# Sums with v in 128 columns of the sequence DFT's PSUM bank: one eviction for both, 120 epochs, seven score banks, a new order of work

## The chip, the cores and the metric

The kernel runs on one core of one Trainium2 chip. The metric is the device time of one launch in microseconds (us), the median of several runs. The core has TensorE (PE in the profile, its weight loads as PEld), VectorE (DVE), ScalarE (ACT), GpSimd (POOL), and DMA queues that are here mostly issued from SyncE (SP). TensorE writes its results to PSUM, which has eight banks of 512 float32 columns on 128 partitions.

## The reference, cut to what matters

Two branches read the same x (2048 tokens, 640 features) and are mixed by a gate. Branch A is a Fourier mixing layer: a DFT over the features and one over the sequence, real part only. Branch B is attention with 32 query heads of 20 features and one shared key and value head.

```python
g = sigmoid((x * gate_w).sum(-1, keepdims=True))
# branch A
a = einsum("bsd,ed->bse", x, dft_hid_re)
b = einsum("bsd,ed->bse", x, dft_hid_im)
y = einsum("ts,bse->bte", dft_seq_re, a) - einsum("ts,bse->bte", dft_seq_im, b)
# branch B, H = 32, Dh = 20
scores = einsum("bhqd,bkd->bhqk", q, k) * Dh ** -0.5
p = softmax(scores, axis=-1)
o = einsum("bhqk,bkd->bhqd", p, v) @ wo
out = g * y + (1 - g) * o
```

## The kernel before, in words

Float32 products are made of two-part operands (a rounded high part and a low part), so that most matmuls run in the fast float32 form. The program has three phases.

**Head.** Projections q, k, v and the gate, then the feature DFT (`ab`, line 137). The first maxima of scores run beside it.

**Main phase.** It runs the list `PLAN`, one character per piece of PE work, in the order in which PE gets it. Four kinds of work are woven together:

- `a`, line 356: a score tile (128 queries by 512 keys) for the softmax's maxima. VectorE reduces it to one column (line 363). There are 1888 in the list.
- `b`, line 824: a score tile transposed (128 keys by 512 queries), with the maximum already subtracted through two more rows. ScalarE takes the exponential into an SBUF tile `pt` (line 834). There are 1920 in the list. Sixteen `pt` tiles exist.
- `y`, line 698: half-height matmuls of the sequence DFT, 320 columns, made with a fast matrix scheme of seven products; a group of 96 half matmuls sums into the first 320 columns of one bank, `F0`. The list has 48 groups (4608 matmuls). At a group's end ScalarE copies the bank (line 726), and GpSimd adds it to what DRAM holds of y (line 753).
- `av`, line 838: the sums with v. One step takes four `pt` tiles (two heads, two query blocks of 512, the same 128 keys) and does four matmuls of 512 columns, each in its own 32 columns of the array, into one bank, `V`. Sixteen steps complete half of a pair of heads; ScalarE copies the bank (line 852, `finish_half`), DMAs write sums and denominators to DRAM.

A score of head 0 and a `y` with digit 0 use rows 0 to 63 of the array, those of head 1 and digit 1 use rows 64 to 127; below, the two halves are called the **two lanes**. A `y` in one lane and scores in the other run at the same time. `av` uses all 128 rows. In the list small letters are scores of head 0 and capitals those of head 1 (first the `a`, then the `b`; the letter's place gives the bank), `0` and `1` are a `y` in that lane, `V` is one `av` step, `-` ends a `y` group. Six banks `S0` to `S5` serve scores, one serves `av`, one serves `y`. Both lanes may not sum into the y bank at once, so a `y` that changes lane waits for a score's eviction behind the last `y` of the other lane (`Halves.run`).

**Tail.** The last 8 `y` groups use two banks and both lanes in turn, with the scores and sums of the last pair of heads between them; the output projection follows.

PE, ACT, DVE and POOL execute in the order in which the program is written; the list therefore also sets the order of the exponentials, the maxima and the copies. POOL also prepares the operands of the coming `y` group (lines 485, 495 and 496 for the DFT matrix, 523 to 527 for x).

Of the kernel before, what the change touches and what calls it, by code (L numbers as in the profile page):

```python
# [8 lines left out]
F32 = mybir.dt.float32  # L9
# [8 lines left out]
P = 128  # L18
S = 2048
# [15 lines left out]
def kernel(  # L35
# [151 lines left out]
    with ExitStack() as c1:  # L187
# [3 lines left out]
        rot = Rot(["B", "V", "F", "B", "F", "A", "A", "A"])  # L191
# [74 lines left out]
        warm = bank("V", "warm")  # L266
# [411 lines left out]
    class Halves:  # L678
# [11 lines left out]
        def run(self, g):  # L690
# [5 lines left out]
            start, stop = grp[k] == 0, grp[k] == (6 if one else 3) * NT - 1  # L696
            grp[k] += 1
            mm = nc.tensor.matmul(ps[g % len(ps)], w, woven(x), start=start, stop=stop)  # L698
            if one:

                if not start and self.last != g:
                    tc.add_manual_dep(mm.ins, self.mark.ins.name, ORDER, reason="turns with a bank")
                    known["PE"] = max(known["PE"], self.exp)
                if start:
                    known["PE"] = max(known["PE"], known["y"])
                self.last, self.mark = g, None
# [50 lines left out]

    def f_stream():
# [5 lines left out]
        for g, (n, k) in enumerate(GROUPS):  # L764
            ps = [bank("F0", f"y_{n}_{k}")[:, :HALF]]
            if g >= GMAIN:
                ps.append(bank("S5", f"y_{n}_{k}_1")[:, :HALF])
            y0 = y_in(n, k)
            grp = [0, 0]
            for sh in range(2):  # L770
                h, l = c_ops.pop((g, sh))
                load_c(g + 1, sh)
                for j in range(SJ):
# [12 lines left out]
                    if jj == NT - 1:  # L786
                        ended.append({"n": n, "k": k, "ps": ps, "y": y0})
# [11 lines left out]
    known = {"PE": -1, "ACT": -1, "y": -1}  # L799
# [36 lines left out]

    def av_mm(ps, g, t, kc, first, last):
        nc.tensor.matmul(ps[32 * g : 32 * g + 32, :], vsb[:, kc, :], t, start=first, stop=last)  # L838

    def av_step(p, qh, kc):  # L840
        if kc == 0:
            av[qh] = bank("V", f"av_{p}_{qh}")
# [7 lines left out]
    def finish_half(p, qh):  # L850
        ob = op.tile([P, ROW], F32, name="ob")
# [8 lines left out]
        if p == LAST:  # L860
            sm = op.tile([P, 16], F32, name="sm")
            ts = slice(qh * S // 2, (qh + 1) * S // 2)
            for hh in range(2):
                move(sm[64 * hh : 64 * hh + 64], sum_d[2 * p + hh, ts].rearrange("(s t) -> s t", t=16))
            later(4, finish_last, ts, sm)
        elif qh == 1:
            sm = op.tile([P, 32], F32, name="sm")
            move(sm, sum_d[2 * p : 2 * p + 2].rearrange("h (s t) -> (h s) t", t=32))
            later(24, finish_sums, p, sm)
# [11 lines left out]
    def finish_last(ts, sm):  # L881
# [13 lines left out]
    SCORES = "abcdefABCDEFghijklGHIJKL"  # L895
    PLAN = (
        "g1b111id11k1111l1a11hc1111d1k1111lAhCk00LD000A0H000K0I0F00D0000HA00KVJbgKCfVVlkCAHdV0KC00H00A000J00F"
        "0K0I00B00A0J0000K0F000IB0V0IF00HEajV1h11dk111a11lc11h111dk1111a1l1111bi11ej11-VdBiGKfVV1fk1111gb1c11"
        "1j1l1e1111g1111hdi11111f1k11a1dHVaKbFdIVVLbI0J000A00E00L000HC0000G00DE00L0000I00B0G00D00LE0VDlgBKcVA"
        "H0000E00I00D0LA00000B000KClDVV1i11dl11h11e1111a1id11111fe1h11iGVIf-HjeAV1f1h11e1g11d11i1l111b11e1g11"  # L900
        "c1d1111fh1V1HikDa1ViDhFEgV0H00FG00E00JI000000BF000GdEVVDlKGbcV0K00BG000I0F00JE0000000HA0I00L0D000E0H"
        "00A000CJ000FVVLc111a1jh1111e1l11c111j1ab11k11f111JiV-dhAEIfVVeI1a1l1bj111111e11i1l111g1111dbi111k11f"
        "VeHiDFgV11i1dGkFbVaJ00KF000H0C00G00D000EL0000H00CA000J00LVCjGfBeVVBl0GEC000J0000LB000000GE000J00I00L"
        "000BAVl1b11i11a111ej1111lh11111cgd111el1VfjACKbVVC-eAjHlVd1he1111gf1i1111j1h111e11a11i1111fj1e1111hG"
        "cVkBgLCdVgB000I0FJ000K0G0000BC0F000DVVL00C000J0A0H0000E0L0CJ0000GB00000FK000D0C000AH000KVVGc1k11d1h1"
        "1f111g111c1kd111111h1fg1cKV-ViElaBJV1fG1e1j1c11h11111fg1j1e11b111i1111g1l1dV1aL11dbiKVjClGBeVLc0H00A"
        "K0D00000L0CH0000A00K0J0000F0I0B000E00AD0VVG0E00JB0000I0000LA00K000DB0C00FgVVIal111h1d1e1111ia1111l11"
        "1j11b111iegF-VeIaBlJVfgK1d1Ch1VeJ1a11i1h1f111111je111i111ah1l1111dk11cVjFIKbaVVGe0H00C0FD00000A00K00"
        "B0CVVAj0B00K0L000C00DG000K00000H00FG0C00J00000E0H00FG00c0D0hKVbIf111j11k111ac111b1j111f1k1a1VVlB1g1e"
        "c1JV-EgdBIlVc1j11f1h11g1e1111i11d1fh1111g1e11i1111jh11fAVF0H000A0J0C00K00F0H0000000JAKcVAjeLIbVVBCkL"  # L910
        "gdV0E0L0C00J0000AH000EL000I0000D0BG000L00E00I00JA0VDegiFHV1ai111k11fh1111dg1111i1fe1111hd11VHeiFd-GV"
        "VAj111lc11e11h111aj1111li1b11111e1j111a1fiHVa11iHlkDVVK0F00J0000BI000GE0F000D00HC000AeVVI00AJ00000FK"
        "B00I000G0D00L0000EI0B000000AD00F0KVVGej1111b1lc1111g11e1j11b1l11111ia1e-JVaIBlKjVV1dkb1111l111g1c111"
        "1je111h111la1c111de11h11GlVadHClKVhA0LD000I00K00B000G00F000JC0B000EVVehCdGLVhE0G000C0J0F000H0E00G0I0"
        "0000D0F00H0EG000000IDViEa1Dl11hVa1h111d111l11kc111g11bd1f111kIVDeIb-fGVV1b1g1f1k11id1111b11g1lk11111"
        "c1111da111h11liEVfGBjiEVJ00B0I000E0GF00000J0B000C00E00GdFVVkCJ0AB000L00000E0I00J000GF00000HC00J00E0A"
        "00L0VVaLeJIbVJak1111cbl111j11111a1ei11l1111h1j1GcVVA-dIhKfVIahd111111l1k11c11g1b11j11f11c1111k1b1g11"
        "dl1VFBgcDkVV0I0E0J0000BG000F0C000K0D00H0GVBigDKfVA000JE00L0CH0000G000D0000KF0H000C0A000J0K00L00BVEaB"
        "1lj11iV1aj1111bif1111k111a1j11111bc-kFVVIeLbaJVf11h111dge1111i11f1h1111j11g1c11k11b1fV1e1bG1fIjVVJ00"
        "0FI00H0AE0000J00L0000I0AH000J0E000F0000GCVaFjKiBVlD0K0A0hC00000L0J000E0AB0000C00F0kDVVIe111fhg1d1111"  # L920
        "11i1e1h111la11d11c11kHVV-ihEJaFV1c11h11a1k11jf1111b11i11e1g1111j1l1c1111haVH0A0000I0F0J000E0H00G00C0"
        "0FJ0VJcFgBkVg0CF0eJH0VVE0HFj0cG0VdLBeIgVCj0B000G0E00L0ID000000AH00F0K000I00D00HVBl11d1ik1111a1f1h111"
        "11i1de11g1h111-fIVViLEbaJV1l1e111jb11g1c1l11111kd11b111g1f11c11kd111gVaL00IK0bDVbCeGjFVV00EJL0000C00"
        "AH0000K0D0L0I0000BG000E00JF0000H0C000G0K000D0F0B0000I000ADeVVgB1d11i11k1f11g111h1c1111d11e11lg1-IbVV"
        "1ch1a111k1l1111dc111h11g11k1f11j1111bcV1bD1kfiG1VcJeBlGVFi00K0AHD0000I0L00000E0G000B0J0CVVCbjgELVdIA"
        "0000H0K00F0I0D000H0G000EF00000ID0B00000E00AClVVkB1a1l111j1i11e111hf11111a11jec111HlVbeGDcL-VVJf111ei"
        "11g1b111j11f11ik1a111111h1j1f1i11ea11VCkJfAhVdIL000BG00E00000CJ00000FB000AEjVVA000H0D00K0F00I0A00H00"
        "J0K0000C000FH0G0000D00C0KVJgIeHlVVHc11g11fk11d111h11i1a11111f1ed111bG-iVViDBkaLVKd1bl111g1c11k111d1l"
        "111h1g11c11111e1d1l11h1cVbjFKcGVjBK0000F0I0A00J0000BE0L00CVVCKfHjaVkC0H0F0A0J000K00C0000H0000FJ0G00K"
        "0C0000B00D00F0G0I00EVVKfc1j111gh11111e1l11d1c111g11k1b11DlVV-jFhKcAV1h11c1k11lad11111h1i11e111a1l111"  # L930
# [77 lines left out]
    def next_v():  # L1008
        st = taken["V"] - LAG
        taken["V"] += 1  # L1010
        if st >= 0:
            av_step(*STEPS[st])
            if STEPS[st][2] == NT - 1:
                finish_half(*STEPS[st][:2])
# [114 lines left out]
```

## Time and profile before

| | |
|---|---|
| Runs shown | 1712.6, 1713.92, 1716.32 us; median 1713.92 us |
| Profiled execution, its own time | 1714.89 us |
| Its span in the trace | 1713.1 us |
| Granted TensorE clock | 1.0 of full speed in all 40 slices |
| PE / DVE / ACT / POOL busy share | 99% / 84% / 70% / 48% |

The profile has one row per group of instructions: the line, the engine, the operation, what it writes and reads, the count, the busy time of the group and the mean time of one. A float32 matmul of `av` leaves two records, one for each of its two passes, so 2048 matmuls of `av` stand as x4096. Records of PE overlap, since a record lasts from the start to the drain and the next matmul starts before that; the distance between starts is what counts.

In the views by time a row gives the start, the length from the first start to the last end, the engine and the group; what stands in square brackets at the end is idle time of that engine before the row and what ended it.

### The profile page before, as it was taken

What the parts mean: (1) busy time and instruction counts of PE and PEld (TensorE: products, weight loads), DVE (VectorE), ACT (ScalarE), POOL (GpSimd) and SP (SyncE); (2) the same over time, 40 slices, a digit from 0 to 9 for tenths busy, and PEclk for the clock granted to TensorE, in tenths of its full rate; (3) what the DMA queues carried; (4) which work ended last, traced back from release to release, by engine and by line L of the source; (5) the groups of instructions that cost most, each with busy time, mean ns of one, the idle gap of its engine ahead of it and who ended that gap; (6) DMA issues with size and microseconds to landing.
All of it is one profiled execution on the core that took longest, in us unless ns stands there. A gap on an engine that the chain in (4) does not pass through costs nothing.

```text
span 1713.1 us, 40813 instructions
## 1 busy us (share of the span) xinstructions
PE 1703.6 (99%) x16342; PEld 1194.6 (70%) x16342; DVE 1440.0 (84%) x2355; ACT 1199.3 (70%) x2337; POOL 817.6 (48%) x559
## 2 busy tenths in 40 slices
PE   9999999999999999999999999999999999999998
PEld 8899986666666666666666666666666666667788
DVE  5779999999898889898998989998989998855264
ACT  5732257777787777877777777778777777877731
POOL 1011344553646464647566565565564453542252
PEclk9999999999999999999999999999999999999999
DMA  8863433343344444435344544353443332325667
GB/s 292 240 182 117 141 109 122 103 134 106 121 136 138 122 134 126 141 110 165 128 144 135 170 126 138 115 151 116 139 145 118 99 111 89 107 79 182 200 214 248
DMA packets 131002, 243.88 MB, mean 142 GB/s; under 512 B 26356, under 2 KB 77556, under 8 KB 128292
## 3 DMA queue, kind: packets, MB, share of 16 engines
q1 hardware_dynamic: 130012, 238.00, 44.2%
q0 software_dynamic: 800, 3.28, 0.6%
q8 instruction: 128, 2.10, 0.5%
q14 instruction: 62, 0.51, 0.1%
HBM read 194.62 MB, written 50.86 MB: 143 GB/s over the span
## 4 chain that ended last, share of the span: by engine, by line
PE 90%; DMA 3%; issue 3%; POOL 2%; DVE 1%; SPq 0%; ACT 0%; POOLq 0%; DVEq 0%
PE av L838 27%; PE y L698 19%; PE a L356 16%; PE b L824 16%; PE ab L137 7%; PE q L126 1%; PE q L128 1%; PE q L127 1%; DMA oraw<-rx_d 1%; POOL ya L753 1%; POOL oraw L632 1%; SPq L118 0%; DMA out_dram<-oy 0%; PE o L128 0%; POOL yt L748 0%
## 5 line engine op out<-in xcount | busy, mean ns | idle before, releaser
L363 DVE TENSOR_REDUCE mx<-a 128x1 f32<-128x512 f32 x2048 | 1265.5, 681 | 126.4 <-PE a L356 88.5
L834 ACT ACTIVATE pt<-b 128x512 f32<-128x512 f32 x2048 | 1055.4, 613 | 291.7 <-PE b L824 171.8
L698 PE MATMUL y<-x,ch 64*128 64x320 f32 x3584 | 706.8, 299 | 0.9 <-ACT yt L726 0.9
L356 PE MATMUL a<-ks,qs 60*128 60x512 f32 x2048 | 705.1, 411 | 0.3 <-ACT half L570 0.3
L824 PE MATMUL b<-qs,ks 62*128 62x512 f32 x2048 | 672.2, 408 | 0.1
L698 PEld LDWEIGHTS y<-x,ch 64*128 64x128 f32 x3584 | 545.3, 186 | 51.0 <-issue 31.4
L838 PE MATMUL av<-pt,vsb 128*32 128x512 f32 x4096 | 512.8, 601 | 0.0
L698 PE MATMUL y<-x,cl 64*128 64x320 f32 x1792 | 496.1, 297 | 0.0
L356 PEld LDWEIGHTS a<-ks,qs 60*128 60x128 f32 x2048 | 345.8, 184 | 123.3 <-ACT pt L834 64.2
L824 PEld LDWEIGHTS b<-qs,ks 62*128 62x128 f32 x2048 | 336.9, 184 | 132.6 <-DVE mx L363 74.2
L485 POOL TENSOR_TENSOR craw<-craw 128x1024 f32<-128x1024 f32 x80 | 189.4, 2368 | 266.3 <-DMA craw<-in_cre_dram 116.2
L698 PEld LDWEIGHTS y<-x,cl 64*128 64x128 f32 x1792 | 310.4, 186 | 5.6 <-issue 5.0
L496 POOL TENSOR_TENSOR cl<-craw,ch 128x1024 fp32r<-128x1024 f32 x98 | 232.1, 2368 | 8.1 <-PE a L356 0.3
L838 PEld LDWEIGHTS av<-pt,vsb 128*32 128x32 f32 x4096 | 98.1, 108 | 183.5 <-issue 172.3
L495 POOL CAST ch<-craw 128x1024 fp32r<-128x1024 f32 x98 | 101.6, 1037 | 137.0 <-PE y L698 91.4
L137 PE MATMUL ab<-wh,xh 64*128 64x320 f32 x640 | 124.2, 297 | 1.3 <-DVE both L571 0.8
L137 PE MATMUL ab<-wl,xh 64*128 64x320 f32 x640 | 123.8, 296 | 0.0
L137 PE MATMUL ab<-wh,xl 64*128 64x320 f32 x640 | 123.7, 296 | 0.0
L753 POOL TENSOR_TENSOR ya<-yt,ya 128x320 f32<-128x320 f32 x64 | 60.5, 960 | 86.9 <-ACT yt L726 86.3
L570 ACT ACTIVATE half<-ab 128x320 f32<-128x320 f32 x64 | 28.0, 437 | 104.6 <-PE ab L137 95.8
L137 PEld LDWEIGHTS ab<-wl,xh 64*128 64x128 f32 x640 | 89.4, 186 | 0.0
L137 PEld LDWEIGHTS ab<-wh,xl 64*128 64x128 f32 x640 | 89.4, 185 | 0.0
(88 smaller groups left out, 1089.0 us busy)
## 6 DMA issues: line engine op xcount, KB each, us to landing
craw<-in_cre_dram SPq DMA_DIRECT2D x96, 512.0 KB
craw<-in_cim_dram SPq DMA_DIRECT2D x96, 512.0 KB
xr<-x_d SPq DMA_DIRECT2D x88, 320.0 KB
qs<-qh_d SPq DMA_DIRECT2D x64, 160.0 KB
x_d<-both SPq DMA_DIRECT2D x64, 160.0 KB
ya<-y_d SPq DMA_DIRECT2D x64, 160.0 KB
y_d<-ya SPq DMA_DIRECT2D x64, 160.0 KB
xr<-in_xT_dram SPq DMA_DIRECT2D x20, 256.0 KB
```

Source lines behind the costliest of these rows:

```text
L137: nc.tensor.matmul(ps, w[r], woven(x[r]), start=(i == 0 and k == 0), stop=(i == n - 1 and k == 2))
L356: nc.tensor.matmul(ps, qs[p][b : b + 60, qb * P : (qb + 1) * P], woven(ks[b : b + 60, c * ROW : (c + 1) * ROW]), start=True, stop=True,)
L363: return nc.vector.tensor_reduce(mx[p][:, hh, qb, c : c + 1], ps, axis=AX.X, op=ALU.max)
L485: eng.tensor_tensor(raws[0], raws[0], raws.pop(1), op=PRODUCTS[GROUPS[g][0]][0][1])
L495: eng.tensor_copy(h, raw)
L496: eng.tensor_tensor(l, raw, h.bitcast(F32), op=ALU.subtract)
L570: nc.scalar.activation(half, ps[0], AF.Copy, scale=sg)
L698: mm = nc.tensor.matmul(ps[g % len(ps)], w, woven(x), start=start, stop=stop)
L753: nc.gpsimd.tensor_tensor(ya, yt, ya, op=how)
L824: nc.tensor.matmul(ps, ks[b : b + 62, kc * P : (kc + 1) * P], woven(qs[p][b : b + 62, qc * ROW : (qc + 1) * ROW]), start=True, stop=True,)
L834: halves.scored(nc.scalar.activation(t, ps, AF.Exp, scale=SCALE), n)
L838: nc.tensor.matmul(ps[32 * g : 32 * g + 32, :], vsb[:, kc, :], t, start=first, stop=last)
```

## The change

- The bank of `y` is now one tile, `shared`, for the whole main phase: columns 0 to 319 hold `y`, columns 320 to 447 hold the sums with v. Bank `V` becomes `S6`, so that scores have seven banks in the list.
- The sums with v go through streams, one for each pair of heads, query block of 512 and head: 15 x 4 x 2 = 120 in the main phase. A `V` in the list is now one `pt` tile: four matmuls of 128 columns, one for each quarter of the tile's 512 queries, each in its own 32 columns of the array (line 862 of the changed kernel). The list has 1920 of them in place of 478 steps; two more steps than before are thereby done ahead of the tail, which does 32 in place of 34 (its first block of two goes).
- A `-` now ends an epoch: ScalarE copies the 128 columns of the sums (line 877) and then the 320 columns of `y` (line 890). There are 120, each with 16 `V` and with 16 to 72 `y`. The first matmul into the bank behind it waits for the second copy. A `y` group spans several epochs, so its copies are partial sums; GpSimd adds the second and later ones (line 892, 72 adds), and the addition to DRAM's y follows when the group's 96 matmuls are done.
- The exponentials come in runs by head: in a stream all 16 key blocks of one head and query block.
- The list is new. In the sums' copy to DRAM each row goes in pieces of 128 columns; the number of DMAs is the same.

The core of the diff:

```diff
-            ps = [bank("F0", f"y_{n}_{k}")[:, :HALF]]
+            if g < GMAIN:
+                ps = [shared["F"][:, :HALF]]
...
+    def next_v(end):
+        st, kc = divmod(taken["V"], NT)
+        p, qc, hh = STREAMS[st]
+        taken["V"] += 1
+        t, slot = pt.pop((hh, kc, qc))
...
+        acc = shared["F"][:, HALF : HALF + VW]
+        fresh = shared["fresh"]
+        for g in range(4):
+            mm = nc.tensor.matmul(
+                acc[32 * g : 32 * g + 32], vsb[:, kc], t[:, g * VW : (g + 1) * VW], start=fresh, stop=end
+            )
+            if shared["fresh"]:
+                opened(mm)
...
+    def opened(mm):
+        shared["fresh"] = False
+        if shared["out"]:
+            tc.add_manual_dep(mm.ins, shared["out"].ins.name, ORDER, reason="shares a bank")
...
+    def epoch():
...
+        ev = nc.scalar.activation(
+            obs[hh][:, qc * VW : (qc + 1) * VW], shared["F"][:, HALF : HALF + VW], AF.Copy
+        )
...
+        if grp:
+            ev = y_part(*grp)
...
+    def y_part(done, _, info):
+        t = op.tile([P, HALF], F32, tag="yu" if "t" in info else "yt", name="ypart")
+        ev = nc.scalar.activation(t, info["ps"][0], AF.Copy)
+        if "t" in info:
+            nc.gpsimd.tensor_tensor(info["t"][0], info["t"][0], t, op=ALU.add)
...
-    SCORES = "abcdefABCDEFghijklGHIJKL"
+    SCORES = "abcdefgABCDEFGhijklmnHIJKLMN"
...
-        "g1b111id11k1111l1a11hc1111d1k1111lAhCk00LD000A0H000K0I0F00D0000HA00KVJbgKCfVVlkCAHdV0KC00H00A000J00F"
...
+            p, r = divmod(nb, 64)
...
-        block = 2 if kk in (0, NT - 1) else 4 * (kk % 2)
+        block = 0 if kk == 0 else 2 if kk == NT - 1 else 4 * (kk % 2)
```

More of the change, by code (lines that the diff above doesn't have):

```diff
@@ L263, in kv_turn @@
             )
-        warm = bank("V", "warm")
+        warm = bank("S6", "warm")
         for _ in range(WARM):
@@ L695, in run @@
             k = 0 if one else g
-            start, stop = grp[k] == 0, grp[k] == (6 if one else 3) * NT - 1
+            start, stop = grp[k] == 0, grp[k] == 3 * NT - 1
+            if one:
+                start, stop = shared["fresh"], end
             grp[k] += 1
@@ L699, in run @@
             if one:
-                if not start and self.last != g:
+                if start:
+                    opened(mm)
+                elif shared["y"] and self.last != g:
                     tc.add_manual_dep(mm.ins, self.mark.ins.name, ORDER, reason="turns with a bank")
                     known["PE"] = max(known["PE"], self.exp)
-                if start:
-                    known["PE"] = max(known["PE"], known["y"])
+                shared.update(y=grp, mm=mm)
                 self.last, self.mark = g, None
@@ L798 @@
     ptfree = [(-1, k) for k in range(16)]
-    known = {"PE": -1, "ACT": -1, "y": -1}
+    known = {"PE": -1, "ACT": -1}
     last = {}
@@ L835, in b_unit @@
         pt[(hh, kc, qc)] = t, (n, slot)
+    STREAMS = [(p, qc, hh) for p in range(LAST) for qc in range(4) for hh in range(2)]
+    def next_v(end):
[3 more added lines that the diff above has]
+        t, slot = pt.pop((hh, kc, qc))
+        known["PE"] = max(known["PE"], slot[0])
+        acc = shared["F"][:, HALF : HALF + VW]
[5 more added lines that the diff above has]
+            if shared["fresh"]:
+                opened(mm)
+        shared["mm"] = mm
+        ptfree.append(slot)
@@ new lines, in y_part, with finish_head, part, cols @@
+    def y_part(done, _, info):
[3 more added lines that the diff above has]
+            nc.gpsimd.tensor_tensor(info["t"][0], info["t"][0], t, op=ALU.add)
+        else:
+            info["t"] = [t]
+        if done == 6 * NT:
+            y_out(info)
+        return ev
+    def finish_head(p, hh):
+        h = 2 * p + hh
+        ob = obs.pop(hh)
+        def part(ap, g):
+            return ap.rearrange("d (q g t) -> d g q t", g=4, t=VW)[:, g]
+        def cols(ap):
+            return ap.rearrange("d (q t) -> d q t", t=VW)
+        for g in range(4):
+            move(part(sum_d[h : h + 1], g), cols(ob[32 * g + DH : 32 * g + DH + 1]))
+            move(part(oT_d[h * DH : (h + 1) * DH], g), cols(ob[32 * g : 32 * g + DH]))
+        if hh == 1:
+            sm = op.tile([P, 32], F32, name="sm")
+            move(sm, sum_d[2 * p : 2 * p + 2].rearrange("h (s t) -> (h s) t", t=32))
+            later(24, finish_sums, p, sm)
@@ L1005, in next_b, with last_v @@
         taken["b"][g] += 1
         ready()
[L1008 to L1014, printed above, removed]
-    for what in PLAN:
-        if what == "V":
-            next_v()
-        elif what == "-":
-            y_evict()
-            known["y"] = taken["b"][0] + taken["b"][1] - 1
-        elif what in "01":
-            halves.run(int(what))
-        else:
-            kind, s = divmod(SCORES.index(what), 6)
-            if kind >= 2:
-                if min(state) >= NA and sum(taken["b"]) % 2 == 0:
-                    tick()
-                next_b(kind - 2, f"S{s}")
-            else:
-                if taken["a"] % 2 == 0:
-                    tick()
-                waits(f"S{s}", -1)
-                a_half(kind, f"S{s}", True)
-                taken["a"] += 1
+    def last_v(n):
+        for _ in range(n):
+            st = next(steps)
+            av_step(*st)
+            if st[2] == NT - 1:
+                finish_half(*st[:2])
@@ new lines @@
+    for part in PLAN.split("-"):
+        ends = max(part.rfind(x) for x in "01V")
+        for i, what in enumerate(part):
+            if what == "V":
+                next_v(i == ends)
+            elif what in "01":
+                halves.run(int(what), i == ends)
+            else:
+                kind, s = divmod(SCORES.index(what), 7)
+                if kind >= 2:
+                    if min(state) >= NA and sum(taken["b"]) % 2 == 0:
+                        tick()
+                    next_b(kind - 2, f"S{s}")
+                else:
+                    if taken["a"] % 2 == 0:
+                        tick()
+                    waits(f"S{s}", -1)
+                    a_half(kind, f"S{s}", True)
+                    taken["a"] += 1
+        if shared["y"] or not shared["fresh"]:
+            epoch()
@@ L1051 @@
         y_evict()
-        for _ in range(block):
-            next_v()
+        last_v(block)
         for f in BEFORE.get(kk, ()):
             f()
-    old = STEPS[-LAG:]
     for _ in range(2):
@@ L1070 @@
         if i == 0:
-            for st in old:
-                av_step(*st)
-            finish_half(*old[-1][:2])
+            last_v(2)
         n, k = divmod(i, 4)
```

252 lines of the change are left out of this document (139 added, 113 removed).

## The prediction

> **What bounds the kernel now.** The page's busy times come first:
>
> ```profile
> span 1713.1 us, 40813 instructions
> PE 1703.6 (99%) x16342; PEld 1194.6 (70%) x16342; DVE 1440.0 (84%) x2355; ACT 1199.3 (70%) x2337; POOL 817.6 (48%) x559
> ```
>
> PE is never long idle, but a busy PE isn't a full one: a record counts while one lane rests. So I read the timeline next, for the distance between starts. First a piece in which one lane does y and the other scores:
>
> ```profile
> 611.10 0.29 PE L698 MATMUL y<-x,ch 64*128 64x320 f32 x1
> 611.18 0.38 PE L824 MATMUL b<-qs,ks 62*128 62x512 f32 x1
> 611.24 0.29 PE L698 MATMUL y<-x,cl 64*128 64x320 f32 x1
> 611.37 0.29 PE L698 MATMUL y<-x,ch 64*128 64x320 f32 x1
> 611.40 0.38 PE L824 MATMUL b<-qs,ks 62*128 62x512 f32 x1
> 611.50 0.30 PE L698 MATMUL y<-x,ch 64*128 64x320 f32 x1
> 611.62 0.38 PE L356 MATMUL a<-ks,qs 60*128 60x512 f32 x1
> 611.64 0.30 PE L698 MATMUL y<-x,cl 64*128 64x320 f32 x1
> 611.84 0.48 PE L356 MATMUL a<-ks,qs 60*128 60x512 f32 x1
> ```
>
> A y takes its lane 0.135 us (611.10 to 611.64 is four of them), a score 0.219 (611.18 to 611.84 is three). Next the sums with v, between stretches that use both lanes for scores:
>
> ```profile
> 600.19 1.93 PE L838 MATMUL av<-pt,vsb 128*32 128x512 f32 x16
> 602.04 0.48 PE L356 MATMUL a<-ks,qs 60*128 60x512 f32 x1
> ...
> 603.11 1.06 PE L838 MATMUL av<-pt,vsb 128*32 128x512 f32 x8
> 604.10 0.48 PE L356 MATMUL a<-ks,qs 60*128 60x512 f32 x1
> 604.11 0.48 PE L824 MATMUL b<-qs,ks 62*128 62x512 f32 x1
> 604.42 0.38 PE L356 MATMUL a<-ks,qs 60*128 60x512 f32 x2
> 604.64 0.39 PE L824 MATMUL b<-qs,ks 62*128 62x512 f32 x2
> 604.96 1.06 PE L838 MATMUL av<-pt,vsb 128*32 128x512 f32 x8
> ```
>
> and its weight loads:
>
> ```profile
> 600.18 0.16 PEld L838 LDWEIGHTS av<-pt,vsb 128*32 128x32 f32 x8 [0.23 <-issue]
> 600.64 0.13 PEld L838 LDWEIGHTS av<-pt,vsb 128*32 128x32 f32 x4 [0.30 <-issue]
> 601.07 0.13 PEld L838 LDWEIGHTS av<-pt,vsb 128*32 128x32 f32 x4 [0.30 <-issue]
> ```
>
> Passes follow each other at 0.43 us (600.64, 601.07), and four matmuls in four quarters of the array share each pass. Two passes make a step: 0.857 (0.43 is 0.4286 when the starts are followed over a run). One step takes 603.11 to 604.10, 0.99, so 0.14 goes by behind it; two take 1.85. Six scores, three to a lane, take 604.10 to 604.96, 0.86, of which 3 x 0.219 = 0.66 is work and 0.20 goes by until the next sums start. Going into the sums and out costs 0.34 us for each run of them.
>
> With this the main phase can be added up. It begins and ends at these rows:
>
> ```profile
> 232.34 0.38 PE L356 MATMUL a<-ks,qs 60*128 60x512 f32 x1
> ...
> 1543.18 0.46 ACT L726 ACTIVATE yt<-y 128x320 f32<-128x320 f32 x1
> 1543.50 0.63 ACT L834 ACTIVATE pt<-b 128x512 f32<-128x512 f32 x1
> 1543.79 0.40 PE L698 MATMUL y<-x,ch 64*128 64x320 f32 x2 [0.92 <-ACT yt L726]
> ```
>
> 1311.4 us. The list has 478 steps in 344 runs, hence 345 stretches between. Steps: 478 x 0.857 = 410. Runs: 344 x 0.34 = 117. A stretch lasts as long as its longer lane. All lanes' work is 4608 x 0.1355 + 3808 x 0.219 = 1458, half of it 729; the lanes' differences, counted stretch by stretch in the list, add up to 75, and half of that, 37, is lost: 767 (766.5 unrounded). Together 1293. Only 18 us remain for all waits for banks and engines, although the waits' view reports far more idle time of weight loads:
>
> ```profile
> PEld b L824 <- DVE mx L363: 74.2, 92, 0.9
> PEld a L356 <- ACT pt L834: 64.2, 77, 0.9
> ```
>
> That idle time lies at the drains and in the shorter lane. So the main phase is bound by PE's packing. DVE is the next wall: 1888 maxima in the list by 0.618 each, from
>
> ```profile
> L363 DVE TENSOR_REDUCE mx<-a 128x1 f32<-128x512 f32 x2048 | 1265.5, 681 | 126.4 <-PE a L356 88.5
> ```
>
> (1265.5/2048), are 1167 us, which leaves room of 144 us.
>
> **The lanes.** On PE, at the end of the first half of the second pair of heads (y, a, b and av as in the text above), before:
>
> ```order
> L698 MATMUL y_1_4359<-x_0_3514,cl 128x320
> L824 MATMUL b_3_2_1_4674<-qs_863,ks 128x512
> L356 MATMUL a_1_4678<-ks,qs_864 128x512
> L824 MATMUL b_0_2_0_4681<-qs_863,ks 128x512
> L356 MATMUL a_1_4685<-ks,qs_864 128x512
> L838 MATMUL av_0_4062<-pt,vsb 32x512 x8
> L698 MATMUL y_1_4359<-x_0_2343,ch 128x320
> L824 MATMUL b_0_3_0_4707<-qs_863,ks 128x512
> ```
>
> and now, on PE at the end of an epoch in the same part (L700 is now y, L838 b, L862 the sums):
>
> ```order
> L700 MATMUL shared<-x_0_3514,cl 128x320
> L862 MATMUL shared<-pt,vsb 32x128 x16
> L838 MATMUL b_9_1_0_4455<-qs_863,ks 128x512
> L356 MATMUL a_1_4459<-ks,qs_864 128x512
> L838 MATMUL b_0_1_1_4462<-qs_863,ks 128x512
> L838 MATMUL b_1_1_1_4466<-qs_863,ks 128x512
> L356 MATMUL a_0_4470<-ks,qs_864 128x512
> L838 MATMUL b_10_1_0_4473<-qs_863,ks 128x512
> L862 MATMUL shared<-pt,vsb 32x128 x24
> ```
>
> The epoch closes with four `V` (16 matmuls), six scores cover the copies, six `V` open the next. The new list has 1920 `V` in 352 runs, 353 stretches, with the same y and scores; the lanes' differences add up to 29 in place of 75. Half of the change, -22.8 us, is the gain. Runs: 8 more here and one fewer in the tail, 7 x 0.34 = +2.4. The two steps that the tail no longer does are in the 1920, so as work they cancel.
>
> **The sums in short passes.** 1920 `V` are 480 old steps, 411.4 us if a pass of 128 columns took a quarter of 0.4286, 0.107. No row shows such a pass with 32-column weights. From above the nearest is the warm-up, 128 columns with 128-column weights:
>
> ```profile
> 4.47 0.50 PE L268 MATMUL warm<-ident 128*128 128x128 f32 x3
> ...
> 4.80 0.28 PE L268 MATMUL warm<-ident 128*128 128x128 f32 x1
> ```
>
> (0.50 - 0.28)/2 = 0.111. If a float32 pass takes two cycles for a column where a y takes one, the two known distances, 320c + g = 0.1355 and 1024c + g = 0.4286, give c = 0.000416 and a fixed gap g = 0.0023, and 256c + g = 0.109. This lies nearer to the row with the same weights, so I take it: 2 x 0.109 x 1920 = 418.6, +7.2 us; ends +0 (0.107) and +16 (0.1115).
>
> **The shared bank.** ScalarE now has two copies at each `-`, in front of the six scores' exponentials. On ACT, before, at the same half's end:
>
> ```order
> L834 ACTIVATE pt<-b_3_2_1_4674 128x512
> L834 ACTIVATE pt<-b_0_2_0_4681 128x512
> L852 ACTIVATE ob<-av_0_4062 128x512
> L834 ACTIVATE pt<-b_0_3_0_4707 128x512
> L834 ACTIVATE pt<-b_1_2_0_4716 128x512
> ```
>
> and now at the epoch's end:
>
> ```order
> L848 ACTIVATE pt<-b_8_1_0_4415 128x512
> L877 ACTIVATE ob<-shared 128x128
> L890 ACTIVATE ypart<-shared 128x320
> L848 ACTIVATE pt<-b_9_1_0_4455 128x512
> L848 ACTIVATE pt<-b_0_1_1_4462 128x512
> ```
>
> Two copies stand in a row, and the first `V` or y behind the six scores waits for the second. How long that chain is, another eviction shows:
>
> ```profile
> 676.46 0.48 PE L356 MATMUL a<-ks,qs 60*128 60x512 f32 x1
> 676.60 0.60 ACT L852 ACTIVATE ob<-av 128x512 f32<-128x512 f32 x1 [0.34 <-PE av L838]
> 677.09 1.57 ACT L834 ACTIVATE pt<-b 128x512 f32<-128x512 f32 x3
> 677.31 0.16 PEld L838 LDWEIGHTS av<-pt,vsb 128*32 128x32 f32 x8 [0.34 <-ACT ob L852]
> ```
>
> The copy starts 0.14 after the first score behind the sums, and PE goes on 0.11 after its end. A 512-column copy holds ACT for 0.49 (676.60 to 677.09), a 320-column one for 0.32 (1543.18 to 1543.50), so 128 columns hold it for about 0.15. Chain: 0.14 + 0.15 + 0.46 + 0.11 = 0.86; six scores give 0.86. They just cover it where ScalarE is free. 106 of the 120 epochs have 3 and 3 scores (or one more) and then `V`. An exponential that stands ahead costs up to 0.49 more: three take 1.57 at 677.09, one instruction of 512 columns lasts 0.60, and (1.57 - 0.60)/2 = 0.49. With one epoch in seven so hit: 120 x 0.07 = +8 us (an estimate; ends 0 and 59). Behind the waiting matmul all of PE's later work is queued, and behind that ACT and DVE.
>
> **POOL** gets 72 more adds, of 0.96 us each by
>
> ```profile
> L753 POOL TENSOR_TENSOR ya<-yt,ya 128x320 f32<-128x320 f32 x64 | 60.5, 960 | 86.9 <-ACT yt L726 86.3
> ```
>
> 69 us on an engine that is idle for half of the span. It now waits for ScalarE 120 times in its own order, ahead of the operand work for the next group. That work has a quarter to half a group of lead, so I cost it at nothing; without that lead it would be up to 0.96 x 72 = 69 us.
>
> **The sum** against the profiled execution, 1714.9 us: -22.8 + 2.4 + 7.2 + 8 = -5.2, 1709.7. That execution lies 1.0 above the median of the runs shown, so the forecast for the median is **1708.7 us**.
>
> **The rivals.**
>
> *Weights don't come in time (slower).* The four loads for a pass take 0.13 us (600.64), longer than a pass of 0.107 lasts. If the next pass waits for them to end, a `V` takes 0.26, 1920 of them 499, +88 over the old price, and the time is 1714 - 12 + 88 = 1790 (12 is what the other terms bring: 22.8 - 2.4 - 8). Against it: at 600.18 eight loads for two passes are done within 0.16, so a load is pipelined. The change loses its gain from a pass of 0.1104 on (12.4/3840 = 0.0032 above 0.1071). Chance 0.14.
>
> *Issue.* A `V` has 16 records where a quarter step had 4. The densest longer stretch before is
>
> ```profile
> 96.25:100.20 3.95, 3.95 (x64) 3.95 (x62) 0.91 (x3) 1.05 (x3) 0.86 (x1) 1.00 0.97 193
> ```
>
> 126 records in 3.95 us, 0.031 each. If PE could not be fed faster, a `V` would take 0.50 in place of 0.214, +549 us: 2252. Against it, eight loads and four matmuls start together at 600.18 to 600.19. The Trainium skill, "TensorE: Matmul & The Clock Gate", section "Back-to-back issue gap", has a rule on this side: a sustained stream of load and matmul pairs at 128 columns spaces its matmuls by about 81 ns. As an estimate by that page, eight in a row would make a `V` 0.65 us and the time some 2540 us; the four that share each pass at 600.64 speak against applying it here. Chance 0.04.
>
> *Evictions (slower).* If an exponential stands in the way at every epoch, 120 x 0.49 = 59 in place of 8: 1760. From a mean wait of 0.11 us on there is no gain left. Chance 0.13.
>
> *No gain in the packing.* The slack of a stretch shrinks from 0.22 to 0.08 us, so a score that waits for its bank now delays the stretch: 0.1 us in each of 247 stretches with y would be +25, 1734. The seventh bank speaks against it. Chance 0.10.
>
> *A better fit.* The epochs hide entirely and seven banks remove half of the 18 us of waits: -17 more, 1692. Chance 0.15.
>
> **Chances.** The forecast, 1700 to 1716, has 0.44. The range is 1690 to 1745: it takes in the better fit, the packing and part of the evictions, and leaves out the long passes, issue and the worst evictions. Faster by over 0.2% (3.4 us, about what a measurement of this kernel can tell from no change): most of the forecast's cases and the better fit, 0.49. Within: 0.20. Slower: 0.31.
>
> **What would show it.** In the new trace: weight loads of the sums 0.109 us apart from pass to pass (a wait there means the first rival); the six scores behind an epoch 0.86 us from the first to the next sums, with ScalarE's two copies ending 0.11 ahead; the main phase at about 1308 us (1311.4 with the same terms, and the two steps from the tail). The forecast is wrong if the passes exceed 0.1104, if the epochs' gaps average over 0.11, or if DVE or ACT ends more waits than before inside the y stretches.

## The result and the profile after

The changed kernel takes **1787.05 us** (median of 4 runs, 1777.64 to 1789.07) against 1713.7 us before (4 runs): ratio 1.0415, 95% interval 1.0376 to 1.0453. It is slower by 73 us, outside the forecast range (1690 to 1745), where the forecast had it slightly faster (1708.7). The profiled execution took 1786.79 us.

Of the page after, the busy times, PE's and the clock's slices, and the groups of `b` and of the sums:

```profile
span 1785.0 us, 64060 instructions
...
PE 1706.0 (96%) x27862; PEld 1493.9 (84%) x27862; DVE 1439.7 (81%) x2355; ACT 1227.8 (69%) x2499; POOL 877.9 (49%) x631
...
PE   9999999999999999998896999899979899899999
...
PEclk9999999999999999999898999899989999999999
...
L838 PE MATMUL b<-qs,ks 62*128 62x512 f32 x2048 | 658.0, 402 | 67.6 <-DMA qs<-m_d 67.2
...
L862 PE MATMUL shared<-pt,vsb 128*32 128x128 f32 x15360 | 497.2, 277 | 0.1
```

PE was 99% busy before and is 96% busy now. The holes lie in some slices from the 19th on, and in four of these the clock dips as well. The matmuls of the sums with v wait for nothing (0.1 us in all). The idle time stands before `b`. The waits' view names it (engine, line and tile, what was waited for; us in total, times, longest):

```profile
POOL ypart L892 <- ACT ypart L890: 236.1, 35, 19.6
...
PE b L838 <- DMA qs<-m_d: 67.2, 11, 16.4
```

Such a wait of PE is not among the waits of before at all. `qs<-m_d` is the transfer that puts a pair's maxima into the two extra rows of `qs` that `b` reads. The chain that feeds it for a pair of heads is: VectorE joins the last maxima (line 369) and transposes them (line 377), GpSimd makes two parts `ms` of them (lines 378 and 379), SP issues a store to DRAM and then four loads into `qs`. With nobody in the way it looks like this in the timeline after (start, length, engine, instruction):

```profile
743.34 0.29 DVE L369 TENSOR_REDUCE mxr<-mx 128x32 f32<-128x128 f32 x1
...
744.74 0.20 DVE L377 STREAM_TRANSPOSE mt<-mxr 128x32 f32<-128x32 f32 x1
...
745.00 0.21 POOL L378 CAST ms<-mt 128x32 fp32r<-128x32 f32 x1 [5.15 <-DVE mt L377]
745.29 0.25 POOL L379 TENSOR_TENSOR ms<-mt,ms 128x32 fp32r<-128x32 f32 x1
745.57 0.32 SPq L118 DMA_DIRECT2D m_d<-ms  x1
...
748.29 2.51 SPq L118 DMA_DIRECT2D qs<-m_d  x4
...
752.09 0.48 PE L838 MATMUL b<-qs,ks 62*128 62x512 f32 x2 [0.21 <-DMA qs<-m_d]
```

From 743.34 to 752.09 is 8.75 us: POOL was waiting for `mt` (5.15 us), SP issued the store at once, and the loads when it had landed. Here PE lost 0.21 us. The list decides how much time there is: it is the number of scores between a pair's last `a` and its first `b`. Counted in the two lists, with the pairs numbered from 0, it was 49 to 59 for pairs 3 to 13 before (39 and 32 for pairs 2 and 14), some 16 to 20 us at the prediction's prices; now it is 18 to 35 for pairs 3 to 14, some 6 to 13 us. The longest hole shows what else stood in the chain. First POOL, in the timeline after, from the transposed maxima to their parts:

```profile
937.59 0.20 DVE L377 STREAM_TRANSPOSE mt<-mxr 128x32 f32<-128x32 f32 x1
...
939.29 0.88 POOL L892 TENSOR_TENSOR ypart<-ypart 128x320 f32<-128x320 f32 x1
940.24 0.87 POOL L756 TENSOR_TENSOR ya<-ypart,ya 128x320 f32<-128x320 f32 x1
941.06 2.38 POOL L485 TENSOR_TENSOR craw<-craw 128x1024 f32<-128x1024 f32 x1
943.51 1.04 POOL L495 CAST ch<-craw 128x1024 fp32r<-128x1024 f32 x1
944.62 2.34 POOL L496 TENSOR_TENSOR cl<-craw,ch 128x1024 fp32r<-128x1024 f32 x1
946.91 0.21 POOL L378 CAST ms<-mt 128x32 fp32r<-128x32 f32 x1
```

and then SP's queue, up to PE's next `b`:

```profile
948.20 0.64 SPq L118 DMA_DIRECT2D sum_d<-ob  x1
948.88 0.80 SPq L118 DMA_DIRECT2D oT_d<-ob  x1
...
955.09 0.77 SPq L118 DMA_DIRECT2D oT_d<-ob  x1
955.97 0.42 SPq L118 DMA_DIRECT2D m_d<-ms  x1
...
957.52 2.52 SPq L118 DMA_DIRECT2D qs<-m_d  x4
...
960.38 0.76 PE L838 MATMUL b<-qs,ks 62*128 62x512 f32 x1 [16.41 <-DMA qs<-m_d]
```

The maxima were there at 937.8. POOL came to them at 946.9, behind an addition of a partial y, one of a whole y and the operand work, and SP issued their store at 956.0, behind the eight stores of a finished head, 7.8 us for all of them. PE stood for 16.4 us. In the windows' view (us; start and end, length, busy time and count of PE, PEld, DVE, ACT and POOL, granted clock, DMA share, GB/s) the hole goes on after its end:

```profile
944.00:960.00 16.00, 0.00 (x0) 0.00 (x0) 0.36 (x1) 0.00 (x0) 3.29 (x4) 0.63 0.49 120
960.00:965.00 5.00, 4.62 (x38) 3.88 (x42) 1.38 (x2) 3.15 (x6) 0.00 (x0) 0.50 0.02 3
965.00:975.00 10.00, 10.00 (x192) 8.46 (x188) 7.58 (x13) 7.40 (x16) 7.81 (x5) 0.99 0.15 37
```

For 5 us behind it PE works at half of its clock: 38 records, where the next 10 us have 192. The Trainium skill, "TensorE: Matmul & The Clock Gate", section "What's actually happening", says that an idle stretch of about 3.4 us halves TensorE's clock and that about as long a busy one restores it; the 0.50 and the 0.99 agree. By the clock's records in this trace it halved 4.1 us after PE's last work and came back 4.7 us after its next.

The nine holes longer than 1 us, each at a pair's first `b`, add up to 66.8 us. Followed over the clock's records, PE was besides busy for 38 us at the half clock, which loses some 19 us (an estimate: half of that time). The theory: **the list lost the lead of the maxima; the queues of POOL and SP, through which the rows pass, make it worse.** The first rival: the short passes or the epochs' copies cost the time. The second: the wait is only the place where another lack shows, and PE would wait elsewhere if it were gone.

### The profile page after: what moved, and what is told of

Its sections match the earlier page's. It is cut to its first block, busy times and chain, and to the rows that moved or that the text cites. A ratio compares the mean times of both kernels' runs of the same rounds, so it can differ in the third digit from the quotient of the medians.

```text
span 1785.0 us, 64060 instructions
## 1 busy us (share of the span) xinstructions
PE 1706.0 (96%) x27862; PEld 1493.9 (84%) x27862; DVE 1439.7 (81%) x2355; ACT 1227.8 (69%) x2499; POOL 877.9 (49%) x631
## 4 chain that ended last, share of the span: by engine, by line
PE 85%; DMA 6%; POOL 4%; DVE 2%; SPq 1%; issue 1%; ACT 0%; POOLq 0%; DVEq 0%; ACTq 0%
PE shared L862 24%; PE shared L700 16%; PE b L838 15%; PE a L356 14%; PE ab L137 6%; PE y_F L700 3%; DMA qs<-m_d 2%; PE av L918 2%; SPq L118 1%; PE q L126 1%; PE q L128 1%; PE q L127 1%; POOL cl L496 1%; DMA m_d<-ms 1%; DVE mx L363 1%; POOL craw L485 1%
## 5 line engine op out<-in xcount | busy, mean ns | idle before, releaser
L838 PE MATMUL b<-qs,ks 62*128 62x512 f32 x2048 | 658.0, 402 | 67.6 <-DMA qs<-m_d 67.2
L356 PE MATMUL a<-ks,qs 60*128 60x512 f32 x2048 | 677.1, 399 | 0.3 <-ACT half L570 0.3
L700 PE MATMUL shared<-x,ch 64*128 64x320 f32 x3072 | 666.9, 304 | 0.3 <-ACT ypart L890 0.2
L700 PEld LDWEIGHTS shared<-x,ch 64*128 64x128 f32 x3072 | 504.2, 188 | 18.2 <-issue 12.3
L862 PE MATMUL shared<-pt,vsb 128*32 128x128 f32 x15360 | 497.2, 277 | 0.1
L862 PEld LDWEIGHTS shared<-pt,vsb 128*32 128x32 f32 x15360 | 401.4, 110 | 87.2 <-issue 52.8
L700 PE MATMUL shared<-x,cl 64*128 64x320 f32 x1536 | 463.0, 301 | 1.5 <-ACT ypart L890 1.2
L838 PEld LDWEIGHTS b<-qs,ks 62*128 62x128 f32 x2048 | 347.8, 187 | 109.2 <-issue 54.8
L700 PEld LDWEIGHTS shared<-x,cl 64*128 64x128 f32 x1536 | 289.1, 188 | 6.0 <-issue 2.4
L892 POOL TENSOR_TENSOR ypart<-ypart 128x320 f32<-128x320 f32 x72 | 62.6, 870 | 236.3 <-ACT ypart L890 236.1
```

The source lines that it names most:

```text
L356: nc.tensor.matmul(ps, qs[p][b : b + 60, qb * P : (qb + 1) * P], woven(ks[b : b + 60, c * ROW : (c + 1) * ROW]), start=True, stop=True,)
L838: nc.tensor.matmul(ps, ks[b : b + 62, kc * P : (kc + 1) * P], woven(qs[p][b : b + 62, qc * ROW : (qc + 1) * ROW]), start=True, stop=True,)
L862: mm = nc.tensor.matmul(acc[32 * g : 32 * g + 32], vsb[:, kc], t[:, g * VW : (g + 1) * VW], start=fresh, stop=end)
L892: nc.gpsimd.tensor_tensor(info["t"][0], info["t"][0], t, op=ALU.add)
```

## The experiments

Ratios are to the kernel before, timed on the same chip, with 95% intervals.

**More lead (undo one part).** The number of `a` in the DFT stage ahead of the list goes up, so that the whole stream of maxima is further ahead; the list is otherwise as changed.

```diff
-    LEAD = 16
+    LEAD = 24
```

> The changed kernel with the maxima 24 tiles per head ahead of the main phase in place of 16, nothing else. Counted in the list, the distance from the last a of a pair of heads to the first b of that pair grows from 18 to 35 scores to 47 to 60, as in the kernel before (49 to 59). Theory (lead): the 67 us in which PE waits for the rows of maxima, and the half clock behind them, go; 1705 to 1720 us, of which up to 10 are 16 more maxima of 0.62 us in the stage of the feature DFT, where DVE is busy all the time. Rival (short passes or more instructions): stays above 1770. Rival (two copies per epoch): stays above 1750.

1723.12 us, ratio 1.0052 (1.0040 to 1.0065). The lead is now 47 to 85 scores. Of 67.2 us of waits for the rows 2.7 us are left, beside three short waits for the low part of the DFT matrix from POOL:

```profile
PE shared L700 <- POOL cl L496: 5.3, 3, 1.9
...
PE b L838 <- DMA qs<-m_d: 2.7, 2, 2.1
```

64 of the 73 us are gone with the same sums, copies and banks. The 16 additional maxima make the DFT stage some 8 us longer (the first `b` starts at 242.5 in place of 234.1).

**Rows of another pair's maxima (take the wait away).** Each pair's extra rows get the maxima of the pair before, which are long there. The part that is changed: the number that is subtracted in the exponent. It cancels between the sums and their denominators as long as no exponential leaves its range, which other data need not grant, so this is a measurement and not a version to use.

```diff
-        for hh in range(2):
-            for i in range(2):
-                r = 64 * hh + 60 + i
-                move(qs[p][r : r + 1]...
+        for pr in ([0] if p == 0 else []) + ([p + 1] if p + 1 < NPAIR else []):
+            for hh in range(2):
+                for i in range(2):
+                    r = 64 * hh + 60 + i
+                    move(qs[pr][r : r + 1]...
```

> The changed kernel, but the rows of maxima for a pair of heads are written from the maxima of the pair before it, so that they are there a whole pair early. The output is then not the reference's; the number of DMAs is the same but for the first and the last pair. Theory (lead): 1703 to 1716 us, no PE wait for these rows, granted clock back to 1.0. Rivals (short passes, copies): within 10 us of the changed kernel, 1777 to 1790.

1714.2 us, ratio 0.9995 (0.9986 to 1.0004). With the same list and the same instructions, but without the wait, all 73 us of the loss are gone. The longest waits of PE that are left:

```profile
PE shared L701 <- POOL cl L497: 6.8, 5, 1.9
...
PE shared L701 <- POOL ch L496: 5.3, 1, 5.3
```

So there is something in the second rival: holes of some 12 us for POOL's operand work, which the long holes of the changed kernel covered.

**The kernel before with less lead (do that part alone).** LEAD 8, and 16 `a` put into the list near its pairs' ends; 512-column sums, six banks, one copy as before. The lead is 11 to 31 scores. One of the list's lines, with the inserted `d` and `E`:

```diff
-    LEAD = 16
+    LEAD = 8
...
-        "1j1111hfVjElHCaVL00C00H0G00E0D000L000IB00K0000AFjVVL0D0G00K0B00000CL0D000G00H0E000F000I0A000J0BVVHa1"
+        "1j1111hfVjElHCadEVL00C00H0G00E0D000L000IB00K0000AFjVVL0D0G00K0B00000CL0D000G00H0E000F000I0A000J0BVVH"
```

> The kernel before, with the maxima 8 tiles per head ahead in place of 16 and the 16 maxima that are then missing put in by pairs near the end of the list. The distance from a pair's last a to its first b falls from 49 to 59 scores to 11 to 31. Theory (lead): it gets slower by 30 to 100 us, with PE waits for the rows of maxima at nearly every pair, although its passes, banks and copies are the old ones. Rivals (the loss lies in the new passes or copies): within 10 us of the kernel before.

1809.21 us, ratio 1.0553 (1.0539 to 1.0568). The same wait appears in a kernel that has nothing of the change:

```profile
PE b L824 <- DMA qs<-m_d: 57.5, 11, 12.6
```

The loss of 94 us is larger than the 57.5 of this row. The mean granted clock is 0.978, as in the changed kernel, where before it was 1.0: by the clock's records PE was busy for 57 us at the half clock, which loses some 28 us by the same estimate.

**The kernel before with short passes.** Each step's four matmuls of 512 columns become sixteen of 128.

```diff
+        ts = []
...
-                av_mm(av[qh], 2 * hh + j, t, kc, kc == 0, kc == NT - 1)
+                ts.append((2 * hh + j, t))
...
+        for q in range(4):
+            for g, t in ts:
+                cs = slice(128 * q, 128 * q + 128)
+                nc.tensor.matmul(
+                    av[qh][32 * g : 32 * g + 32, cs],
+                    vsb[:, kc, :],
+                    t[:, cs],
...
```

> The kernel before, with each step's four matmuls of 512 columns cut into sixteen of 128 columns, in the same bank and order of tiles. Passes of 0.109 us: 512 steps x (8 x 0.109 - 2 x 0.4286) = 512 x 0.015 = +8 us, 1721. Passes of 0.1115 us (the warm-up row): +18 us. If a pass had to wait for its loads, 0.13 us: +94 us. If the issue of instructions were the bound, 0.031 us for each of the 64 records of a step's 32 matmul and 32 load records: +580 us.

1722.73 us, ratio 1.0045 (1.0031 to 1.0059): +8.0 us for 512 steps, where the prediction's price gives 512 x 4 x (2 x 0.109 - 0.2143) = +7.6. The short passes of the first rival are out, and with them the prediction's slow weights and its limit on issue; the epochs' copies were still there in the first two experiments, in which most or all of the loss was gone.

**The rows' two parts on VectorE.** The two instructions that make `ms` go from POOL to VectorE, past POOL's queue.

```diff
-        nc.gpsimd.tensor_copy(ms[:, 0], mt)
-        nc.gpsimd.tensor_tensor(ms[:, 1], mt,
+        nc.vector.tensor_copy(ms[:, 0], mt)
+        nc.vector.tensor_tensor(ms[:, 1], mt,
```

> The changed kernel, with the two small copies that make the rows of maxima on VectorE in place of GpSimd, so that they no longer stand behind GpSimd's adds and splits. Theory (lead, with queues adding to it): only the stalls in which GpSimd was late shrink, by about 9 us at the eighth pair and up to 4 at the thirteenth; 1772 to 1785 us, PE still waits for these rows at most pairs. Rival (GpSimd alone makes the rows late): 1710 to 1725, no such wait left.

1805.7 us, ratio 1.0530 (1.0517 to 1.0544): slower than the changed kernel by 19 us. No theory had this. The timeline of this run, POOL and DVE together:

```profile
673.03 2.35 POOL L496 TENSOR_TENSOR cl<-craw,ch 128x1024 fp32r<-128x1024 f32 x1
673.11 0.20 DVE L377 STREAM_TRANSPOSE mt<-mxr 128x32 f32<-128x32 f32 x1
673.35 2.07 DVE L378 CAST ms<-mt 128x32 fp32r<-128x32 f32 x1
675.33 1.54 POOL L523 TENSOR_TENSOR xr<-xr 128x640 f32<-128x640 f32 x1
675.45 1.47 DVE L379 TENSOR_TENSOR ms<-mt,ms 128x32 fp32r<-128x32 f32 x1
676.84 0.68 DVE L363 TENSOR_REDUCE mx<-a 128x1 f32<-128x512 f32 x1
```

A cast of 32 columns, 0.21 us on POOL, takes 2.07 us on VectorE and ends where POOL's instruction ends; the next one does the same. In the six pairs in which POOL ran nothing beside them, the same two took 0.18 and 0.19 us. So VectorE inherits POOL's delay instead of avoiding it, and all maxima queue behind: PE, which never waited for `mx` in the changed kernel, waits 15.8 us for it here, and the rows are hardly earlier. The Trainium skill, "SBUF — State Buffer", section "Who interferes with whom", says that a VectorE cast can enter a mode that uses the ports to SBUF shared with GpSimd, that a VectorE operation with two SBUF inputs contends with a GpSimd instruction that reads SBUF, and that the one that issues first holds the ports for its whole length while the other waits; these rows agree, and the reduction behind them, a kind that the page exempts, takes its usual 0.68 us beside POOL's next cast. PE's waits for the rows in this run, 67.2 us in the changed kernel:

```profile
PE b L838 <- DMA qs<-m_d: 59.7, 11, 15.6
```

**SP's stores later.** The eight stores of a finished head are given out six pieces of work later in the list, so that the rows' store needn't queue behind them.

```diff
-            finish_head(p, hh)
+            later(6, finish_head, p, hh, obs.pop(hh))
```

> The changed kernel, with the eight DMAs of a finished head issued six ticks (twelve maxima, some 8 us) later, so that they do not stand ahead of the rows of maxima in SyncE's queue. Theory (lead, with queues adding to it): the stalls of the ninth, eleventh, thirteenth and fifteenth pair lose 2 to 8 us each, 10 to 18 in all; 1766 to 1780 us. Rival (SyncE alone makes the rows late): 1710 to 1725, no such wait left.

1752.6 us, ratio 1.0222 (1.0208 to 1.0237): 34 us less than the changed kernel, more than was expected. PE's holes for the rows are 38 us in all, the longest 8.7, in place of 66.8 and 16.4:

```profile
PE b L838 <- DMA qs<-m_d: 38.4, 10, 8.7
```

Nearly half of the loss was SP's queue on top of the short lead. The rest is the short lead with what both queues still add: at pairs 7 and 12, where the longest holes are left (8.7 and 8.0 us), POOL still comes to the maxima 5.8 and 4.9 us after they were transposed, and at pairs 7 and 8 SP issues the loads some 7 us after the store, where it was 2.7 above. How much each takes was not separated.

**Sixteen more early `a` in the list.** They are inserted one by one in its first 165 us, where a lane beside `y` has room; the DFT stage stays as it is, and so does the order of all else. The lead is 47 to 68 scores from pair 4 on. The first of them is the `E`:

```diff
-        "hB1c1kl11m11111g1i1h1d111je1VV1kBm1h1lg11j111dbVVVl0K0AG0B0Jm0VVVVV0Cm0I0G000k0AL0000F0JG00I0aDVVVVV"
+        "hB1c1kl11m11111g1i1h1d111je1VV1kBm1h1lg11j111dbVVVl0K0AG0B0Jm0VVVVV0Cm0I0G000k0AL0000F0JG00I0EaDVVVV"
```

> The changed kernel with sixteen more a in the first 165 us of the main list, each in the lane that has scores and in the bank that is free longest; the last sixteen a of the list then find nothing left to do. The distance from a pair's last a to its first b is as in the run with 24 tiles ahead (47 to 60 scores from the fourth pair on), but the stage of the feature DFT is left alone. Theory (lead): no long wait for the rows of maxima, 1708 to 1716 us, 8 to 12 below the run with 24 tiles ahead. Rival (it was the work in the stage of the DFT, not the lead, that mattered there): within 10 us of the changed kernel.

1720.66 us (12 runs, 1716.5 to 1731.2), ratio 1.0039 (1.0024 to 1.0055). The rows' waits go to 1.3 us, but the time is 5 us above what was expected. In the trace, of the fastest of the twelve runs, PE waits for POOL's `cl` twice, 2.4 us in all; what the other runs lose beyond it isn't shown.

**All of these together:** early `a`, rows on VectorE, stores later, and POOL's additions of partial y later as well.

```diff
-            nc.gpsimd.tensor_tensor(info["t"][0], info["t"][0], t, op=ALU.add)
+            later(6, add_part, info["t"][0], t)
...
-            y_out(info)
+            later(6, y_out, info)
```

> The sixteen early a, the copies of the rows on VectorE, the head's DMAs six ticks later, and GpSimd's adds of partial sums six ticks later, so that GpSimd does not wait in its own order for an epoch's end. Theory: besides the lead, the waits of PE for GpSimd's operand tiles (11 us in the run with the maxima of the pair before) go; 1698 to 1708 us, below the kernel before. Rival (the packing brings nothing beyond what the passes cost): 1710 to 1718.

1736.16 us, ratio 1.0116 (1.0102 to 1.0130). A miss: VectorE, held by POOL at ten of the 16 pairs, now stops PE.

```profile
PE a L356 <- DVE mx L363: 7.8, 6, 2.5
...
PE b L838 <- DVE mx L363: 5.3, 7, 1.7
```

**Early `a` and stores later,** with the two diffs shown above, and without VectorE's part:

> The sixteen early a and the head's DMAs six ticks later, the rows' copies on GpSimd as in the change. Theory (SyncE's queue makes what is left of the late rows and late operand tiles): 1708 to 1716 us, about 5 below the run with the early a alone. Rival (what is left comes from GpSimd's own order): no difference from that run, 1717 to 1724.

1714.81 us (12 runs), ratio 0.9994 (0.9984 to 1.0004): 0.45% below early `a` alone, although hardly a wait for the rows was left there. PE's waits for POOL's `cl` in the main phase (2.4 us with early `a` alone) are gone; the rest of the 0.45% was not followed up. One wait for the rows is in this run's trace:

```profile
PE b L838 <- DMA qs<-m_d: 3.7, 1, 3.7
```

It is at pair 8, where POOL comes to the maxima 11 us after they were transposed, behind operand work and the two additions.

**Early `a`, stores later, additions later,** all three as in the diffs above:

> As the run with the early a and the later head DMAs, and GpSimd's adds of partial sums six ticks later. If VectorE's copies of the rows, held by GpSimd, were what made the run with everything slow (16 pairs x 2 to 3.5 us), this one is at 1700 to 1710. If the later adds themselves did harm, it is above 1720.

1709.63 us (10 runs, 1706.8 to 1715.6), ratio 0.9969 (0.9959 to 0.9980): faster than both kernels. In its trace, of the slowest of the ten runs, no wait for the rows is left, and POOL's additions no longer hold its queue:

```profile
POOL ypart L900 <- ACT ypart L890: 7.5, 2, 4.9
```

in place of 198.3 us in 39 waits in the run before it.

**The same with 24 early `a`:**

> As the run before it, with 24 early a in place of 16, so that a pair's first b follows its last a by 59 to 90 scores. If late rows still cost anything there, this is faster by that, 3 to 8 us; if the lead is long enough already, it is the same within 3 us or, by the eight more scores, up to 2 us slower.

1713.43 us (12 runs), ratio 0.9988 (0.9977 to 0.9999). With 16 the rows' waits were already gone; eight more bring nothing.

**Another pair's maxima, stores later, additions later.** The second experiment's rows with the last two edits, and no additional `a`: what the changed list takes when nobody waits for rows or queues.

> As in the run where a pair's rows of maxima are the pair's before (its output isn't the reference's), and besides the stores of sums and the additions of partial y are given out six pieces of work later each. There is then no wait for maxima at all, and PE's waits of 11 us for POOL's low parts of the DFT matrix are the only sizeable rest. Theory: those waits come from the adds (72, up to 0.96 us each) and their wait for ScalarE in POOL's order, which the prediction costed at nothing; with them moved the time falls from 1714 to 1703 to 1710 and the priced terms of the prediction (1708.7) stand. Rival: POOL is late because the matrix's transfers are late, or because of its other work; then the waits stay and the time is 1712 to 1716.

1696.4 us (5 runs, 1695.3 to 1703.1), ratio 0.9905 (0.9889 to 0.9922). That is below both expectations. The waits of 12 us were of the queues' making, as the theory had it; and moving SP's and POOL's work together is worth some 18 us here by the medians (15 by the ratios), not 4 to 11. The page:

```profile
span 1693.9 us, 64031 instructions
...
PE 1683.3 (99%) x27862; PEld 1477.6 (87%) x27862; DVE 1436.8 (85%) x2355; ACT 1226.3 (72%) x2499; POOL 875.7 (52%) x631
...
PE   9999999999999999999999999999999999999999
```

Its main phase begins and ends at these rows, as the prediction took them before:

```profile
231.73 0.38 PE L356 MATMUL a<-ks,qs 60*128 60x512 f32 x1
231.82 0.38 PE L839 MATMUL b<-qs,ks 62*128 62x512 f32 x1
...
1528.51 0.40 PE L701 MATMUL y_F<-x,ch 64*128 64x320 f32 x1 [0.48 <-ACT ypart L891]
```

1296.8 us, where before it was 1311.4 and the prediction had 1308.

## Why the prediction was wrong

**The step that failed** is how the list entered the sum. The sum has no term for a wait for the maxima's rows; it stood at nothing, without a reason given. It took from the list how many steps, runs, `y` and scores there are and how evenly they fill the lanes, and not the order of `a` against `b`. It asked of each queue what the change adds to it, and costed POOL "at nothing" because the operand work "has a quarter to half a group of lead". But the maxima's rows run through POOL and SP too, with a lead of their own, which the change cuts from 16 to 20 us to some 6 to 13, against a chain of 8.75 us with nobody in its way. That no wait for `qs<-m_d` showed before meant only that the lead was enough. The forecast's signs of failure didn't name this wait, nor did any of the rivals.

How the 73 us come about: taking the wait away gives 72.9 (1787.05 to 1714.2). Cutting the lead alone in the kernel before costs 94. Of the loss, 34 us went when SP's stores were moved (1787.05 to 1752.6), which the prediction didn't cost at all: their number is the same, but each of the eight takes SP two and a half to three times as long, as pieces of 128 columns. What this lengthening alone costs was not tried. One store of sums and one of the head's output, before and after:

```profile
850.20 0.24 SPq L118 DMA_DIRECT2D sum_d<-ob  x1
850.49 0.27 SPq L118 DMA_DIRECT2D oT_d<-ob  x1
```

```profile
949.73 0.60 SPq L118 DMA_DIRECT2D sum_d<-ob  x1
950.37 0.77 SPq L118 DMA_DIRECT2D oT_d<-ob  x1
```

The holes of 66.8 us and the some 19 us lost at the half clock are 86 us together. That is more than 73, but the change without these waits is faster than the kernel before: against the 1696.4 us of the last experiment the loss is 91. How the holes divide between the short lead and POOL's lateness isn't settled.

**POOL's additions at nothing** was wrong too, though their price isn't known. With early `a` and later stores, moving them was worth 0.25% (ratio 0.9994 to 0.9969), about 4 us, but a wait of 3.7 us for the rows went with it, so this can be the same chain once more. Where the rows don't matter, with another pair's maxima, PE's 12 us of waits for POOL's operands went when additions and stores were moved together; the two were not separated there.

**The short passes: right.** A run of five `V` has ten passes (40 records), and the next score starts behind it:

```profile
941.93 1.30 PE L862 MATMUL shared<-pt,vsb 128*32 128x128 f32 x40
943.16 0.48 PE L356 MATMUL a<-ks,qs 60*128 60x512 f32 x1
```

1.23 us less the exit of 0.14 is 0.109 a pass, as forecast, and the kernel before with such passes lost 8.0 us. The rivals of slow weights and of issue didn't come about. The 81 ns between matmuls of the Trainium skill ("TensorE: Matmul & The Clock Gate", section "Back-to-back issue gap") don't hold for these: four matmuls share each 0.109 us.

**The epochs' copies: too dear.** Followed over the 106 epochs with six scores, the time beyond the scores' own work is 0.203 us in the last experiment, where the prediction's ordinary gap was 0.20: well under 1 us in all, in place of 8. Only eight of them took over 0.95 us, where the prediction had 0.86, so ScalarE was free at nearly all.

**The lanes and the banks: right, and better than forecast.** Without the waits the main phase is 14.6 us shorter than before; the forecast had 3 us. The copies account for 7 of the difference of 11. As much again comes from the stretches with `y`: followed over the trace, the time that they take beyond the longer lane and the 0.20 is 10 us, where it was 17 before. (Some 3 us go the other way: a run of `V` is left in 0.151 us, where it was 0.141.) That is what the rival of the better fit said (1692); it came out at 1696.4 in a version that has no waits for the rows. Whether the seventh bank or the evener lanes did it was not separated.

The version with early `a`, later stores and later additions, at 1709.63 us, stands close to the forecast of 1708.7, but that is chance: it needed three edits to get there, and 13 us of the gain are still lost. Its trace, of its slowest run, and that of the last experiment are 20 us apart, and say in part where: 5.4 us in pairs 0 to 2, among which the sixteen early `a` stand, 2.5 in pairs 3 to 14, 8.7 from the first `b` of the last pair on, and 3.4 ahead of the first `b` of all. Why the tail is longer stays open.

## What to carry to other kernels

A list that sets the order of work carries leads that no profile shows while they suffice: when it is replaced, measure for each value that travels through other engines and DRAM how long its chain takes at best, and count that against the new distance from its last producer to its first consumer. A queue's price is who waits behind an instruction, not the instruction's own time, so a wait or a longer store added to a queue is to be held against the shortest lead of all that passes through it. When the distance is too short, repair the order first: moving two of the chain's steps to another engine cost 19 us here, moving other work out of its way brought nearly half of the loss back.

## What the runs showed of the hardware

- A VectorE cast of 128x32 took 2.07 us beside a GpSimd operation of 2.35 us, and ended with it, where GpSimd does it in 0.21 us and VectorE beside an idle GpSimd in 0.18.
- SP took 0.77 us to issue a store whose rows go in pieces of 128 columns, and 0.27 for the same bytes in rows of 512.
- After holes of 12 to 16 us TensorE's granted clock was 0.50 to 0.57 for the next 5 us (0.50 in the window shown above). By the clock's records of the changed kernel, each of the eight holes of 3.5 to 16.4 us brought a stretch at 0.50, of 3.4 to 17.1 us; the hole of 1.2 us brought none.
